# Attention and FFN on one core: the first block of x prepared in halves, and one query chunk of batch 1 loaded by itself

## The chip, the cores and the metric

One core of a Trainium2 chip. The metric is the device time of one execution in microseconds (us); of several runs the median counts. The time before is 242.38 us, the median of 3 runs that lie between 241.73 and 243.09.

## The reference, cut to what matters

```python
def phi(x, c, s):                       # c, s: cos and sin of pi/2 * position / S
    r = np.maximum(x, 0.0)
    return np.concatenate([r * c, r * s], axis=-1)
q_p, k_p = phi(q, cos_w, sin_w), phi(k, cos_w, sin_w)   # (8, 8, 576, 128)
kv  = np.einsum('bhsf,bhsd->bhfd', k_p, v)
z   = np.sum(k_p, axis=2)
num = np.einsum('bhsf,bhfd->bhsd', q_p, kv)
den = np.einsum('bhsf,bhf->bhs', q_p, z)[..., None] + 1e-06
x   = (num / den).transpose(0, 2, 1, 3).reshape(4608, 512)
out = ((x @ w1) * (x @ w2)) @ w3 @ w_out                # w1, w2: 512 x 1024
```

Linear attention over 8 batches (576 rows, 8 heads of 64) makes x, and a multiplicative FFN takes it. The kernel multiplies w3 by w_out once (w34) and works in bf16.

## The kernel before, in words

A batch is cut into five chunks: four of 128 rows (0 to 3) and one of 64 (4). A row index in a chunk is a partition; which row of the batch that is follows from the load, which gives each partition 5 (or 4) neighbouring rows of a head, and output rows go back by the same map. Batch 0's queries and all of batch 7 are loaded whole; the others in two parts, rows 0 to 319 to partitions 0 to 63 and rows 320 to 575 to partitions 64 to 127.

For a batch, the features of k and q (`prep_k`, `prep_q`, both through `features`) are made on VectorE (cosine half, L506, sometimes the sine half, L514) and ScalarE (sine half, L511); `prep_v` copies v beside a column of ones (L526). `kv` multiplies features of k by v over the chunks (L561; for an odd batch chunk 4 comes first), `num` multiplies the transposed features of q by that (L596), `norm` divides (L607 to L609) into `xblk`, and x is transposed into `xT` by TensorE and a copy (`x_tr`, L638 and L639) or by a DMA. Batch 0 has functions of its own in the first 17 us (L956, L964). The FFN takes 512 columns of `xT` at a time (`ffn_groups`): products with w1 and w2 (L685), a copy `asb` (L709, L728, L745), a product of the two on VectorE (L711, L735, L751), then the product with w34 (L768) or seven smaller ones (L878). The FFN's first tile takes its first 128 columns, then the next 128, from `xT` (L696): chunk 0 and chunk 1 of batch 0. `w34_mm` (L483) makes w34 from `w3T`, which `w3_tr` transposes on VectorE (L473) as w3 arrives.

The order of all work on all engines is a table, `PLAN`: a name and its arguments per step, in the order in which the steps are issued. `f t` is the next step of the FFN's generator for tile t, `l b name part` a load, `xt` an `x_tr`, `qt` transposes of q's features, `qy` one half of a copy that a `qt` left out, `idle n` puts n matmuls on zeros (L466) into TensorE's queue. Every engine works through its own steps strictly in that order. Loads are issued by GpSimd (L384), in the same queue as its copies of v. A DMA that GpSimd issues counts on one of eight semaphores in turn, and its issue waits until the DMA that used this semaphore before, eight DMAs earlier, has landed; GpSimd's later steps wait behind it.

```python
    def load_rows(eng, t, rows, half):
        j, span = (5, slice(0, 320)) if half == 0 else (4, slice(320, S))
        eng.dma_start(out=t[ts(half, 64), :, 0:j, :].rearrange("p h j d -> p h (j d)"),
                      in_=rows[:, span, :].rearrange("h (p j) d -> p h (j d)", j=j))
```

Of the kernel before, what the change touches and what calls it, by code (L numbers as in the profile page):

```python
# [16 lines left out]
P = 128  # L17
# [22 lines left out]
f 0; t3 0  # L40
f 0; lg 2 q 0; t3 1; l 2 k 0; l 2 k 1; l 2 q 1; l 2 v 0
f 0
# [25 lines left out]
f 0  # L68
f 0; n 1 0; d 1 0; xt 1 4 A; q 2 0 0; q 2 1; lt 3 v 0; xt 0 4 A
f 0  # L70
f 0; v 2 0 G
f 0
f 0; xt 1 0 V; n 1 1
f 0
# [204 lines left out]


def out_rows(b, c):

    if c < 4:
        return slice(0, 128)
    return slice(64, 128) if b % 2 == 0 else slice(0, 64)


def _angles(nc, pool):

    s_i = pool.tile([P, 2 * NCH], I32, name="s_i")  # L290
    nc.gpsimd.iota(s_i[0:64, 0:5], pattern=[[1, 5]], base=0, channel_multiplier=5)
    nc.gpsimd.iota(s_i[64:128, 0:5], pattern=[[1, 5]], base=320, channel_multiplier=4)
# [30 lines left out]
def kernel(  # L323
# [56 lines left out]

    def load_rows(eng, t, rows, half):

        j, span = (5, slice(0, 320)) if half == 0 else (4, slice(320, S))
        eng.dma_start(out=t[ts(half, 64), :, 0:j, :].rearrange("p h j d -> p h (j d)"),  # L384
                      in_=rows[:, span, :].rearrange("h (p j) d -> p h (j d)", j=j))
# [68 lines left out]
    nc.vector.memset(kp_bufs[0][64:128, 4, :, :], 0.0)  # L454
    nc.vector.memset(raw[0, "v"][64:128, :, 4, :], 0.0)
    clear_rows(0)
# [60 lines left out]
    def prep_k(b, c, n=H, **kw):  # L517
        features(att_of(b)["kp"], raw[b, "k"][:, :, c, :], c, NCH + c if b == 7 else c, n, **kw)

    def prep_q(b, c, n=H, **kw):  # L520
        rows = raw[b, "q"][:, :, c, :] if b > 0 else q0f[:, :, c, :] if c < 4 else q04[:]
        features(att_of(b)["qp"], rows, c, NCH + c if b in WHOLE else c, n, **kw)

    def prep_v(b, c, copy=None):
        R = ROWS[c]
        (copy or nc.gpsimd.tensor_copy)(out=att_of(b)["va"][:R, c, :, 0:D], in_=raw[b, "v"][:R, :, c, :])  # L526

# [72 lines left out]
    def norm(b, c, g0=0, ng=2):  # L600
        rows, R = out_rows(b, c), ROWS[c]
        n4 = att[b]["n"][c][rows, g0:g0 + ng, 0:260].rearrange("p g (h e) -> p g h e", e=65)
        if g0 == 0:
            att[b]["x"][c] = sm.tile([P, 2, 4, D], BF16, name="xblk", bufs=6)
        xblk = att[b]["x"][c]
        den = sm.tile([P, 2, 4], FP32, name="den")
        nc.vector.tensor_scalar_add(out=den[rows, 0:ng], in0=n4[:, :, :, 64], scalar1=1e-6)  # L607
        nc.vector.reciprocal(out=den[rows, 0:ng], in_=den[rows, 0:ng])
        nc.vector.tensor_tensor(out=xblk[rows, g0:g0 + ng], in0=n4[:, :, :, 0:D],  # L609
                                in1=den[rows, 0:ng].unsqueeze(3).to_broadcast([R, ng, 4, D]),  # L610
                                op=ALU.mult)
        divided[0] = xblk[rows, 0, 0, 0:1]
# [20 lines left out]
    def x_tr(b, c, copy=None):  # L633
# [5 lines left out]
        (copy or nc.scalar.copy)(out=x_place(b, c), in_=pst[:, 0:4, 0:R])  # L639

    held = []
    newest = [None]

    def rows_of(b, c, n):
# [6 lines left out]
        upper = out[ds(b * S + 320, 256), :].rearrange("(p j) m -> p j m", j=4)  # L651
        return [h[:, c:c + n, :] for h in ((lower,) if c == 4 else (lower, upper))]

# [22 lines left out]
    def ffn_groups(t):  # L676
# [267 lines left out]
    def kv_first(c, sums, *which):  # L944
# [71 lines left out]
    def store_behind_transposes():  # L1016
# [6 lines left out]
        "f": lambda t: next(ffn[t]), "w": w34_mm, "w3": load_w3, "wo": load_wout, "w12": w12,  # L1023
        "l": load, "lg": gated, "lt": behind_transposes, "lx": behind_division, "lk": behind_feature, "q04": load_q04, "gx": behind_first_x,
        "k": prep_k, "q": prep_q, "v": prep_v,
# [3 lines left out]
        "n": num, "n0": num_first,  # L1029
        "d": norm, "xt": x_tr, "xd": x_dma, "idle": idle_mms, "open": open_ffn, "second": second_pair, "more": more_banks,  # L1030
        "clear": clear_rows, "tw": weight_block, "t3": w3_tr, "st": store_next, "ss": store_by_sync,
# [37 lines left out]
```

## Time and profile before

| | |
|---|---|
| median of 3 runs | 242.38 us (241.73 to 243.09) |
| the profiled execution's own time | 242.14 us |
| its span, first to last instruction | 240.4 us |
| TensorE busy | 234.1 us, 97% of the span |
| VectorE, ScalarE, GpSimd busy | 190.5, 115.6, 79.9 us |
| first FFN product (L685) | 16.90 us |
| `kv` of batch 1 starts (L561) | 50.60 us |
| mean granted TensorE clock | 0.997 |

The span starts at the first instruction, and all times in the trace count from there. A line of the timeline gives start, duration, engine, source line, what is written from what, shape and type, the count of merged instructions, and in square brackets how long the engine had sat idle and what ended that. PE is TensorE, PEld its weight loads, DVE VectorE, ACT ScalarE, POOL GpSimd; POOLq is GpSimd's sequencer.

### The profile page before, as it was taken

How to read it: one execution, taken by the hardware profiler on the slowest of the kernel's cores; microseconds unless marked ns; L12 is line 12 of the kernel's file. 1: busy time of each engine (PE TensorE's matmuls, PEld its weight loads, DVE VectorE, ACT ScalarE, POOL GpSimd, SP SyncE). 2: the span in 40 equal slices, each digit the busy share in tenths (PEclk: the TensorE clock that was granted, in tenths of full speed). 3: DMA queues.
4: the chain of work that ended last, by engine and by line, in shares of the span. 5: the costliest groups of instructions: out<-in, count | busy, mean ns of one | idle time of the engine just before them, and what ended most of it. 6: DMA issues, size and time to landing. Idle time of an engine off the chain costs nothing.

```text
span 240.4 us, 5811 instructions
## 1 busy us (share of the span) xinstructions
PE 234.1 (97%) x2236; PEld 163.5 (68%) x2236; DVE 190.5 (79%) x462; ACT 115.6 (48%) x203; POOL 79.9 (33%) x149
## 2 busy tenths in 40 slices
PE   8999999999999999999999999999999999999993
PEld 2579545476964585798588859966985797484462
DVE  6774596968988937999799889998999788785560
ACT  2754314687755732775384436447164312313321
POOL 8663888541804231221431222021020050363020
PEclk9999999999999999999999999999999999999998
DMA  7999999999999999599999999788457739599824
GB/s 195 194 196 199 183 189 187 198 199 192 182 195 136 142 151 219 76 183 175 148 188 170 152 158 169 131 129 77 80 196 133 110 85 156 130 303 327 253 72 176
DMA packets 84939, 40.48 MB, mean 168 GB/s; under 512 B 48048, under 2 KB 82096, under 8 KB 84912
## 3 DMA queue, kind: packets, MB, share of 16 engines
q0 software_dynamic: 37616, 23.60, 66.9%
q1 hardware_dynamic: 47152, 16.46, 38.8%
q8 instruction: 17, 0.28, 0.4%
q14 instruction: 10, 0.08, 0.2%
q10 hardware_dynamic: 144, 0.07, 0.1%
HBM read 38.80 MB, written 9.44 MB: 201 GB/s over the span
## 4 chain that ended last, share of the span: by engine, by line
PE 92%; DMA 3%; POOL 1%; ACT 1%; DVE 1%; issue 1%; POOLq 0%; DVEq 0%
PE ffnps L685 52%; PE ffnps L878 14%; PE ffnps L768 7%; PE ffnps L483 6%; PE pnum L596 4%; PE pnum L561 4%; DMA vs<-in_v_dram 3%; PE ffnmore L878 1%; PE pst L578 1%; PE ffnps L811 1%; PE ffnps L786 1%; PE pst L638 1%; POOL kf L384 1%; ACT qpT L582 0%; PE pnum L956 0%
## 5 line engine op out<-in xcount | busy, mean ns | idle before, releaser
L685 PE MATMUL ffnps<-xT,w1b 128*128 128x256 bf16 (+2 forms) x448 | 76.2, 303 | 0.2
L685 PE MATMUL ffnps<-xT,w2b 128*128 128x256 bf16 (+2 forms) x448 | 76.2, 303 | 0.0
L685 PEld LDWEIGHTS <-w1b 128*128 128x128 bf16 x448 | 41.1, 98 | 19.3 <-issue 0.8
L685 PEld LDWEIGHTS <-w2b 128*128 128x128 bf16 x448 | 40.8, 98 | 19.7 <-issue 0.2
L745 ACT CAST asb<-ffnps 128x512 bf16<-128x512 f32 x40 | 23.4, 586 | 43.2 <-PE ffnps L685 39.0
L751 DVE TENSOR_TENSOR abT<-asb,ffnps 128x512 bf16<-128x512 bf16 x40 | 27.2, 683 | 15.8 <-PE ffnps L685 15.5
L728 ACT CAST asb<-ffnps 128x512 bf16<-128x512 f32 x24 | 14.1, 586 | 32.9 <-PE ffnps L685 25.9
L609 DVE TENSOR_TENSOR xblk<-pnum,den 128x512 bf16<-128x512 f32 (+1 forms) x38 | 26.2, 691 | 1.5
L735 DVE TENSOR_TENSOR abT<-asb,ffnps 128x512 bf16<-128x512 bf16 x24 | 16.2, 681 | 7.2 <-PE ffnps L685 7.2
L511 ACT ACTIVATE kp<-kf,sinv 128x512 bf16<-128x512 bf16 (+4 forms) x33 | 21.0, 663 | 1.3 <-DMA kf<-in_k_dram 1.3
L878 PEld LDWEIGHTS <-abT 128*128 128x128 bf16 x192 | 18.5, 98 | 3.2
L427 POOL COPY seen<-asb 128x1 bf16<-128x1 bf16 x15 | 3.2, 213 | 50.8 <-ACT asb L728 45.9
L511 ACT ACTIVATE qp<-qs,sinv 128x512 bf16<-128x512 bf16 (+6 forms) x31 | 18.7, 630 | 2.1 <-DMA qs<-in_q_dram 2.1
L596 PEld LDWEIGHTS <-qpT 128*128 128x128 bf16 x320 | 15.1, 98 | 4.3 <-DVE xblk L609 0.4
L768 PE MATMUL ffnps<-w34b,abT 128*128 128x512 bf16 x72 | 17.5, 379 | 0.0
L596 PE MATMUL pnum<-kvs,qpT 128*128 128x65 bf16 x304 | 15.7, 194 | 0.0
L878 PEld LDWEIGHTS <-s 128*128 128x128 bf16 x144 | 13.9, 98 | 1.6
L506 DVE TENSOR_SCALAR kp<-kf,cosv 128x512 bf16<-128x512 bf16 (+1 forms) x40 | 14.5, 384 | 0.4 <-DMA kf<-in_k_dram 0.4
L483 PE MATMUL ffnps<-early,w3T 128*128 128x512 bf16 x64 | 14.3, 379 | 0.0
L384 POOL DMA_DIRECT2D vs<-in_v_dram x16 | 11.9, 750 | 3.5 <-DMA kf<-in_k_dram 1.6
L878 PE MATMUL ffnps<-w34b,abT 128*128 128x256 bf16 x96 | 12.4, 273 | 0.0
L506 DVE TENSOR_SCALAR qp<-qs,cosv 128x512 bf16<-128x512 bf16 (+1 forms) x35 | 12.1, 356 | 0.1
(147 smaller groups left out, 334.1 us busy)
## 6 DMA issues: line engine op xcount, KB each, us to landing
out_dram<-osb SPq DMA_DIRECT2D x9, 256.0 KB, 3.4
kf<-in_k_dram POOLq DMA_DIRECT2D x7, 320.0 KB, 7.0
early<-in_moe_w_dram POOLq DMA_DIRECT2D x16, 128.0 KB, 5.1
qs<-in_q_dram POOLq DMA_DIRECT2D x6, 320.0 KB, 7.6
vs<-in_v_dram POOLq DMA_DIRECT2D x6, 320.0 KB, 7.1
kf<-in_k_dram POOLq DMA_DIRECT2D x7, 256.0 KB, 8.7
qs<-in_q_dram POOLq DMA_DIRECT2D x6, 256.0 KB, 6.8
vs<-in_v_dram POOLq DMA_DIRECT2D x6, 256.0 KB, 8.1
```

What stands on the lines that cost most here:

```text
L384: eng.dma_start(out=t[ts(half, 64), :, 0:j, :].rearrange("p h j d -> p h (j d)"), in_=rows[:, span, :].rearrange("h (p j) d -> p h (j d)", ...
L483: nc.tensor.matmul(acc[:, :], lhsT=w3T[:, lc, :], rhs=woutb[:, lc, :], start=(lc == 0), stop=(lc == 7))
L506: nc.vector.tensor_scalar(out=dst[:R, c, :, 0:D], in0=rows[:R], scalar1=0.0, scalar2=cosv[:R, at:at + 1], op0=ALU.max, op1=ALU.mult)
L511: nc.scalar.activation(out=dst[:R, c, 0:n, D:F], in_=rows[:R, 0:n], func=ACTF.Relu, scale=sinv[:R, at:at + 1], bias=0.0)
L596: nc.tensor.matmul(nt[:, h // 4, ds((h % 4) * 65, 65)], lhsT=qpT[:, h, ds(at, 128)], rhs=kvs[:, h, :], start=True, stop=True)
L609: nc.vector.tensor_tensor(out=xblk[rows, g0:g0 + ng], in0=n4[:, :, :, 0:D], in1=den[rows, 0:ng].unsqueeze(3).to_broadcast([R, ng, 4, D]), ...
L685: nc.tensor.matmul(out, lhsT=w[:, kc, ts(jc, 128)], rhs=x[:, kc, tok], start=(kc == 0), stop=(kc == 3))
L735: nc.vector.tensor_mul(out=abT[:, ts(pair, 2), ts(half, 256)], in0=asb[:].rearrange("p (i n) -> p i n", i=2), in1=bT[:, :].rearrange("p (i ...
L745: nc.scalar.copy(out=asb[:], in_=aT[:, :])
L751: nc.vector.tensor_mul(out=abT[:, jc, :], in0=asb[:], in1=bT[:, :])
L768: nc.tensor.matmul(ops[:, :], lhsT=abT[:, jc, ts(ms, 128)], rhs=w34b[:, jc, :], start=(jc == 0), stop=(jc == 7))
L878: nc.tensor.matmul(into[:, ts(ms, 256)], lhsT=a[:, kc, ts(ms, 128)], rhs=b[:, kc, :], start=(ms == 0 and kc == 0), stop=(ms == 1 and kc == 3))
```

## The change

It has four parts.

1. **The first block of x in halves.** For chunks 0 and 1 of batch 0, `norm` divides by groups of four heads (two instructions of 256 columns in place of one of 512). The new `x_half` transposes two of the four column blocks and copies them to `xT` on ScalarE; it takes the place of `xt 0 0` and `xt 0 1`. Chunk 0's second half uses the PSUM bank `kva`. The FFN's first tile has one step more, after its first product with w1, so that the transposes of chunk 1's halves stand between the first products; three idle matmuls go (one of two ahead of chunk 0's transposes, both ahead of the first product), `qy 0 3 1` moves from VectorE to ScalarE, `xt 0 3` comes one FFN step earlier, and `n 0 3` and `d 0 3` move behind chunk 1.
2. **Memory order.** In batches in two parts, chunk c lies in place `(c + 1) % 5` of the loaded tile and of the five neighbouring rows, so chunk 4 comes first. The angle table's base and the stores follow.
3. **Batch 1's query chunk 3 by itself.** `l 1 q 0; l 1 q 1` become `l1q 0 4`, which loads places 0 to 3 (chunks 4, 0, 1, 2), again as two DMAs; `l1q 4 5` loads place 4 (chunk 3) as two DMAs of 64 columns, behind batch 2's keys and ahead of `l 2 q 1`.
4. **Later features.** `q 1 3` (chunk 3's features, before with both halves on VectorE) moves from ahead of batch 1's keys to behind `d 1 0`, with its sine half on ScalarE, and `q 2 1` moves behind `n 1 1`.

```diff
+BY_GROUP = ((0, 0), (0, 1))
...
+def place_of(c):
+
+    return (c + 1) % NCH
...
-    def load_rows(eng, t, rows, half):
+    def load_rows(eng, t, rows, half, places=(0, 5)):
...
-        eng.dma_start(out=t[ts(half, 64), :, 0:j, :].rearrange("p h j d -> p h (j d)"),
-                      in_=rows[:, span, :].rearrange("h (p j) d -> p h (j d)", j=j))
+        a, b = max(places[0], half), places[1]
+        eng.dma_start(out=t[ts(half, 64), :, a:b, :].rearrange("p h j d -> p h (j d)"),
+                      in_=rows[:, span, :].rearrange("h (p j) d -> p h j d", j=j)[:, :, a - half:b - half]
+                      .rearrange("p h j d -> p h (j d)"))
...
+    def load_q1(*places):
+
+        if places[0] == 0:
+            raw[1, "q"] = ld.tile([P, H, NCH, D], BF16, name="qs", bufs=NRQ)
+        for half in range(2):
+            load_rows(nc.gpsimd, raw[1, "q"], q[1], half, places)
...
-        nc.vector.tensor_tensor(out=xblk[rows, g0:g0 + ng], in0=n4[:, :, :, 0:D],
...
+        n = 1 if (b, c) in BY_GROUP else ng
+        for g in range(0, ng, n):
+            nc.vector.tensor_tensor(out=xblk[rows, g0 + g:g0 + g + n], in0=n4[:, g:g + n, :, 0:D],
...
+    first_x = []
+
+    def x_half(c, half):
+
+        if not first_x:
+            first_x.append(ps_tr.tile([P, 8, 128], BF16, name="pst"))
+        pst = first_x[0]
+        if c == 0 and half == 1:
+            pst = kva[:, :].bitcast(BF16).rearrange("p (k r) -> p k r", k=8)
+        xf = att[0]["x"][c][:].rearrange("p g h d -> p (g h d)")
+        for kc in (2 * half, 2 * half + 1):
+            nc.tensor.transpose(pst[:, kc, :], xf[:, ts(kc, 128)], identb[:])
+        nc.scalar.copy(out=x_place(0, c)[:, ts(half, 2)], in_=pst[:, ts(half, 2), :])
...
+                                if t == 0 and half == 0 and quarter == 0 and i == 0 and w is w1b:
+                                    yield
```

Three places show what this does to the order. The first is GpSimd's queue from batch 1's value loads on (`vs` are values, `kf` keys, `qs` queries; the last two `vs` rows of each are the loads of batch 2's values, and the `va_95` copy behind them is chunk 4 of batch 1's v, which `kv 1` reads first). In brackets stand the semaphores that a row waits for. Before:

```order
L384 DMA vs<-in_v_dram 64x8x320 [waits DMASW3_49]
L384 DMA vs<-in_v_dram 64x8x256 [waits DMASW4_49]
L427 COPY seen<-asb 128x1 [waits Activation_49]
L384 DMA qs<-in_q_dram 64x8x320 [waits DMASW5_49]
L384 DMA kf<-in_k_dram 64x8x320 [waits DMASW6_49,DVE_49]
L384 DMA kf<-in_k_dram 64x8x256 [waits DMASW7_49]
L384 DMA qs<-in_q_dram 64x8x256 [waits DMASW0_49]
L384 DMA vs<-in_v_dram 64x8x320 [waits DMASW1_49,PE_49]
L384 DMA vs<-in_v_dram 64x8x256 [waits DMASW2_49]
L526 COPY va_95<-vs 64x8x64 [waits DMASW3_49]
```

And with the change:

```order
L391 DMA vs<-in_v_dram 64x8x320 [waits DMASW3_49]
L391 DMA vs<-in_v_dram 64x8x256 [waits DMASW4_49]
L442 COPY seen<-asb 128x1 [waits Activation_49]
L391 DMA qs<-in_q_dram 64x8x320 [waits DMASW5_49]
L391 DMA kf<-in_k_dram 64x8x320 [waits DMASW6_49,DVE_49]
L391 DMA kf<-in_k_dram 64x8x256 [waits DMASW7_49]
L391 DMA qs<-in_q_dram 64x8x64 [waits DMASW0_49]
L391 DMA qs<-in_q_dram 64x8x64 [waits DMASW1_49]
L391 DMA qs<-in_q_dram 64x8x256 [waits DMASW2_49]
L391 DMA vs<-in_v_dram 64x8x320 [waits DMASW3_49,PE_49]
L391 DMA vs<-in_v_dram 64x8x256 [waits DMASW4_49]
L542 COPY va_95<-vs 64x8x64
```

Two DMAs stand in the queue that were not there. So batch 2's last value load, ahead of the copy of v, now waits for semaphore 4, which batch 1's own second value load raises when it lands; before it waited for semaphore 2, which batch 1's second key load raises.

The second place is VectorE between the first division and the first product of the FFN (`den` and `xblk` are `norm`'s, from the PSUM tiles `pfirst` and `pnum`; the copy to `qpT` is `qy 0 3 1`). Before:

```order
L608 RECIPROCAL den<-den 128x8
L609 TENSOR_TENSOR xblk<-pfirst,den 128x512
L607 TENSOR_SCALAR den<-pnum 128x8
L608 RECIPROCAL den<-den 128x8
L609 TENSOR_TENSOR xblk<-pnum,den 128x512
L587 COPY qpT_96<-pst 128x4x128
```

And with the change:

```order
L624 RECIPROCAL den<-den 128x8
L627 TENSOR_TENSOR xblk<-pfirst,den 128x256 x2
L623 TENSOR_SCALAR den<-pnum 128x8
L624 RECIPROCAL den<-den 128x8
L627 TENSOR_TENSOR xblk<-pnum,den 128x256 x2
L623 TENSOR_SCALAR den<-pfirst 128x8
```

Each 512-wide division has become two of 256, and the copy is gone from VectorE. The third place is ScalarE at the same point (`qpT` from `pst` is `qy 0 3`, `xT` the transposed x). Before:

```order
L587 COPY qpT_96<-pst 128x4x128
L639 COPY xT<-pst 128x4x128 x2
L709 CAST asb<-ffnps 128x512
L639 COPY xT<-pst 128x4x128
L709 CAST asb<-ffnps 128x512 x3
```

And with the change:

```order
L603 COPY qpT_96<-pst 128x4x128
L671 COPY xT<-pst 128x2x128
L671 COPY xT<-kva 128x2x128
L603 COPY qpT_96<-pst 128x4x128
L671 COPY xT<-pst 128x2x128 x2
L746 CAST asb<-ffnps 128x512
```

Two whole copies of x have become four half ones, with the second half of `qy 0 3` between them.

More of the change, by code (lines that the diff above doesn't have):

```diff
@@ L40 @@
 f 0; t3 0
-f 0; lg 2 q 0; t3 1; l 2 k 0; l 2 k 1; l 2 q 1; l 2 v 0
+f 0; lg 2 q 0; t3 1; l 2 k 0; l 2 k 1; l1q 4 5; l 2 q 1; l 2 v 0
 f 0
@@ L72 @@
 f 0
-f 0; xt 1 0 V; n 1 1
+f 0; xt 1 0 V; n 1 1; q 2 1
 f 0
@@ L517, in prep_k @@
     def prep_k(b, c, n=H, **kw):
[L518 removed]
+        features(att_of(b)["kp"], raw[b, "k"][:, :, c if b == 7 else place_of(c), :], c,
+                 NCH + c if b == 7 else place_of(c), n, **kw)
     def prep_q(b, c, n=H, **kw):
[L521 to L522 removed]
+        rows = raw[b, "q"][:, :, c if b == 7 else place_of(c), :] if b > 0 else q0f[:, :, c, :] if c < 4 else q04[:]
+        features(att_of(b)["qp"], rows, c, NCH + c if b in WHOLE else place_of(c), n, **kw)
     def prep_v(b, c, copy=None):
         R = ROWS[c]
[L526 removed]
+        (copy or nc.gpsimd.tensor_copy)(out=att_of(b)["va"][:R, c, :, 0:D], in_=raw[b, "v"][:R, :, c if b == 7 else place_of(c), :])
     transposed = [None]
@@ L639, in x_tr @@
         (copy or nc.scalar.copy)(out=x_place(b, c), in_=pst[:, 0:4, 0:R])
+    first_x = []
[9 more added lines that the diff above has]
+        nc.scalar.copy(out=x_place(0, c)[:, ts(half, 2)], in_=pst[:, ts(half, 2), :])
+        if half == 1:
+            att[0]["x"].pop(c)
     held = []
@@ L651, in rows_of @@
         upper = out[ds(b * S + 320, 256), :].rearrange("(p j) m -> p j m", j=4)
-        return [h[:, c:c + n, :] for h in ((lower,) if c == 4 else (lower, upper))]
+        at = place_of(c)
+        return [lower[:, at:at + n, :]] + ([upper[:, c:c + n, :]] if c < 4 else [])
     def store(eng, osb, g, n, cols=slice(0, DM)):
@@ L1023 @@
         "f": lambda t: next(ffn[t]), "w": w34_mm, "w3": load_w3, "wo": load_wout, "w12": w12,
-        "l": load, "lg": gated, "lt": behind_transposes, "lx": behind_division, "lk": behind_feature, "q04": load_q04, "gx": behind_first_x,
+        "l": load, "l1q": load_q1, "lg": gated, "lt": behind_transposes, "lx": behind_division, "lk": behind_feature, "q04": load_q04, "gx": behind_first_x,
         "k": prep_k, "q": prep_q, "v": prep_v,
@@ L1029 @@
         "n": num, "n0": num_first,
-        "d": norm, "xt": x_tr, "xd": x_dma, "idle": idle_mms, "open": open_ffn, "second": second_pair, "more": more_banks,
+        "d": norm, "xt": x_tr, "xh": lambda b, c, half: x_half(c, half), "xd": x_dma, "idle": idle_mms, "open": open_ffn, "second": second_pair, "more": more_banks,
         "clear": clear_rows, "tw": weight_block, "t3": w3_tr, "st": store_next, "ss": store_by_sync,
```

24 lines of the change are left out of this document (12 added, 12 removed).

## The prediction

> **What bounds the kernel now.** I read the page's totals first, then the groups by line for the time after the start, then the timeline where TensorE still waits.
>
> ```profile
> PE 234.1 (97%) x2236; PEld 163.5 (68%) x2236; DVE 190.5 (79%) x462; ACT 115.6 (48%) x203; POOL 79.9 (33%) x149
> PE 92%; DMA 3%; POOL 1%; ACT 1%; DVE 1%; issue 1%; POOLq 0%; DVEq 0%
> ```
>
> TensorE is busy in all of the span but some 6 us. The groups by line between 22.6 and 236.4 us say where those 6 us are not (last column: idle before the instructions):
>
> ```profile
> L685 PE MATMUL ffnps<-xT,w1b 128*128 128x256 bf16 (+2 forms) x416 | 72.9, 308 | 0.1
> L596 PE MATMUL pnum<-kvs,qpT 128*128 128x65 bf16 x288 | 14.8, 194 | 0.0
> L561 PE MATMUL pnum<-va,kp 128*128 128x65 bf16 x280 | 10.0, 193 | 0.0
> ```
>
> No group shows more than 0.1 us. So behind 22.6 us there is nothing to win, only to lose: what makes TensorE wait there is paid in full. What can be won lies ahead of 22.6 us, and is kept only if every engine that TensorE meets later is early enough too. The change takes no useful matmul away.
>
> **Part 1, the first block of x.** The timeline before, from the first division:
>
> ```profile
> 14.92 0.69 DVE L609 TENSOR_TENSOR xblk<-pfirst,den 128x512 bf16<-128x512 f32 x1
> 15.67 0.40 PE L638 MATMUL pst<-identb,xblk 128*128 128x128 bf16 x4
> 16.10 0.59 ACT L639 COPY xT<-pst 128x512 bf16<-128x512 bf16 x1 [0.48 <-PE pst L638]
> 16.90 0.38 PE L685 MATMUL ffnps<-xT,w1b 128*128 128x128 bf16 x4
> 17.77 0.59 ACT L639 COPY xT<-pst 128x512 bf16<-128x512 bf16 x1 [1.08 <-PE pst L638]
> 18.41 0.38 PE L685 MATMUL ffnps<-xT,w1b 128*128 128x128 bf16 x4
> 22.14 0.42 DVE L639 COPY xT<-pst 128x512 bf16<-128x512 bf16 x1
> 22.16 0.39 PE L685 MATMUL ffnps<-xT,w2b 128*128 128x128 bf16 x4
> 22.61 0.38 PE L685 MATMUL ffnps<-xT,w1b 128*128 128x128 bf16 x4
> ```
>
> The links are division, 0.06 to the transposes, copy, 0.21 to the product. At 18.41 and 22.61 TensorE has waited again for a copy to `xT`, the second time since the four matmuls at 22.16, 0.056 apart, were through at 22.38. A division of 256 columns from PSUM has no row; it lies between half of 0.69 and 0.69, and I take 0.42, since these two VectorE groups show that halving 1024 to 512 saves 0.27:
>
> ```profile
> L858 DVE TENSOR_TENSOR s<-abT,s 128x1024 bf16<-128x1024 bf16 x6 | 4.1, 685 | 0.0
> L858 DVE TENSOR_TENSOR s<-abT,s 128x512 bf16<-128x512 bf16 x13 | 5.5, 424 | 0.4
> L639 ACT COPY xT<-pst x6: 352/586/591, 16.1 to 62.3; 128x512 bf16<-128x512 bf16 x4, 128x256 bf16<-128x256 bf16 x2
> ```
>
> A copy of half the columns takes 0.35 (the third row's minimum). Two transposes take 0.3, by the 0.40 of four less two steps. So the first half is divided at 14.92 + 0.42 = 15.34, transposed by 15.70 and copied by 16.06; the second is divided at 15.69, transposed by 16.06 and copied by 16.42, and the products that need it start at 16.63. Before, they came two matmuls behind 16.90, at 17.01: 0.38 earlier. Two later waits of TensorE go: some 0.1 at 18.41 for chunk 1, whose copies now end at 17.9, when its products start, and 0.23 ahead of 22.61, since `xt 0 3` comes a step earlier. The lead at 22.61 is about 0.7 us; if the halves cost as much as the wholes, only 0.2 remains. The idle matmuls fill a wait and are worth nothing; `qy 0 3 1` on ScalarE ends at 17.0 and is first read at 17.7.
>
> **How much of the lead is kept to 50 us.** VectorE transposes w3 as it lands, and loads don't start earlier because TensorE does:
>
> ```profile
> 33.79 0.41 PEld L483 LDWEIGHTS <-w3T 128*128 128x128 bf16 x3 [0.24 <-DVE w3T L473]
> 37.44 1.30 DVE L473 STREAM_TRANSPOSE w3T<-early 128x512 bf16<-128x512 bf16 x2 [1.93 <-DMA early<-in_moe_w_dram]
> 39.16 1.23 DVE L473 STREAM_TRANSPOSE w3T<-early 128x1024 bf16<-128x1024 bf16 x1
> 40.57 0.42 DVE L582 COPY qpT<-pst 128x512 bf16<-128x512 bf16 x1 [0.18 <-PE pst L578]
> 41.24 0.42 PE L596 MATMUL pnum<-kvs,qpT 128*128 128x65 bf16 x8
> ```
>
> VectorE is tied to a landing at 37.44 and works on to 40.39; the copy at 40.57 can come 0.18 earlier and no more, and the matmul at 41.24, which reads it, begins 0.25 behind its end at 40.99, of which I leave 0.07 for the way between engines. So of 0.7 us 0.18 + 0.18, about 0.35, is kept here; the first row shows a weight load waiting for the same chain at 33.79, where some of it goes already. TensorE would then reach `kv 1` at 50.60 - 0.35 = 50.25.
>
> **Parts 2 and 4.** The new places move the same bytes in runs of the same length. `q 1 3` leaves two instructions of VectorE's queue ahead of `kv 1`, each issued 0.26 behind the last, so features and copies of v there come 0.5 earlier:
>
> ```profile
> 46.40 0.34 DVE L506 TENSOR_SCALAR qp<-qs,cosv 128x512 bf16<-128x512 bf16 x1
> 46.66 0.34 DVE L514 TENSOR_SCALAR qp<-qs,sinv 128x512 bf16<-128x512 bf16 x1
> 50.36 1.04 DVE L526 COPY va<-vs 128x512 bf16<-128x512 bf16 x4
> 50.60 1.44 PE L561 MATMUL pnum<-va,kp 128*128 128x65 bf16 x40
> ```
>
> Without that, the copies at 50.36, read chunk by chunk from 50.85 on, would be late for an earlier `kv 1`. Behind `d 1 0` the features of `q 1 3` are due only for `qt 1 3`, eight FFN steps later; this I cost at nothing. `l 3 q 0`, which overwrites the tile, now waits for them, and GpSimd stands in that wait, but it stood idle there until 59.35 for batch 2's values anyway:
>
> ```profile
> 59.35 0.62 POOL L526 COPY va<-vs 128x512 bf16<-128x512 bf16 x1 [8.64 <-DMA vs<-in_v_dram]
> 66.69 1.27 PE pnum L561 x40
> ```
>
> **Part 3, the added wait.** GpSimd around the same place:
>
> ```profile
> 36.77 0.68 POOL L384 DMA_DIRECT2D qs<-in_q_dram  x1
> 40.56 0.68 POOL L384 DMA_DIRECT2D vs<-in_v_dram  x1 [1.04 <-DMA early<-in_moe_w_dram]
> 44.59 0.68 POOL L384 DMA_DIRECT2D qs<-in_q_dram  x1 [0.31 <-DMA qs<-in_q_dram]
> 46.53 0.74 POOL L384 DMA_DIRECT2D vs<-in_v_dram  x1 [1.27 <-DMA kf<-in_k_dram]
> 47.60 1.80 POOL L384 DMA_DIRECT2D vs<-in_v_dram  x1 [0.33 <-DMA kf<-in_k_dram]
> 49.39 0.62 POOL L526 COPY va<-vs 64x512 bf16<-64x512 bf16 x1
> 49.95 0.76 POOL L384 DMA_DIRECT2D qs<-in_q_dram  x1
> ```
>
> The load at 47.60 is `l 2 v 1`, the copy at 49.39 is `v 1 4`, chunk 4 of batch 1's v, and `kv 1` begins with chunk 4. In the changed queue `l 2 v 1` waits for the landing of `l 1 v 1`. The loads by issue window give the time to landing of three loads: `l 1 q 1` (issued at 36.77), `l 1 v 1` (at 40.56) and `l 2 v 1` itself (at 47.60):
>
> ```profile
> qs<-in_q_dram POOLq DMA_DIRECT2D x1, 256.0 KB, 7.5
> vs<-in_v_dram POOLq DMA_DIRECT2D x1, 256.0 KB, 9.7
> vs<-in_v_dram POOLq DMA_DIRECT2D x1, 256.0 KB, 11.6
> ```
>
> They land at 44.27, 50.26 and 59.20. From the second to the third come six loads of 1728 KB (three of 320, three of 256), so 5.2 ns per KB; `l1q 0 4` is 128 KB smaller, so `l 1 v 1` lands 0.66 earlier, at 49.60. From a landing to the issue that waited for it pass about 0.3 (44.27 to the row at 44.59, which waited for that one). Then `l 2 v 1` is issued at 49.9, which takes 0.68 to 1.80; I take 0.76, the nearest row, at 49.95, beside the same copies of v on VectorE. `v 1 4` starts at 50.65 and takes 0.62, and `kv 1` starts behind it at 51.3 in place of 50.60. TensorE waits about 1.05 us there, and everything behind is **0.7 us later than before**; whatever part 1 won is gone, since this wait hangs on a landing and not on TensorE. By the extremes: 0.6 at the shortest issue, 1.75 at the longest, and -0.35 if `v 1 4` were ready in time. The small loads themselves cost little: they carry what the large ones no longer do, and batch 2's values land within half a microsecond of 59.2, with `kv 2` at 66.69, the row above.
>
> **The sum.** Own time 242.14, plus 0.7 is 242.8; the profiled execution lies 0.24 below the median of the runs, so against that median I predict 242.38 + 0.7 = **243.1 us**.
>
> **Rivals.**
> *The long issue.* The issue at 47.60 took 1.80 while VectorE ran features without a gap. If `l 2 v 1` meets that again, `kv 1` starts at 52.35 and the time is 242.38 + 1.75 = 244.1. For it: VectorE's copies of v become free to run at the same landing that starts this issue, so the two meet each time. Against it: of all issues of this line between 36 and 51 us one alone took so long. The Trainium skill, "SBUF — State Buffer", section "SBUF: two separate sides", says that VectorE and GpSimd share a pair of ports as an exclusive lock, so that GpSimd can't write the descriptors of its DMAs while some VectorE operations run. The row at 47.60 agrees, the row at 49.95 (0.76) only in part; by that rule the issue would end behind the last copy of v, and this rival weighs more.
> *The gain is kept.* `v 1 4` decides only if it ends later than 50.25; a wait for `l 1 v 1` that ended by 48.8 would spare it. Then the time is 242.38 - 0.35 = 242.0, or 241.7 if all 0.7 us survive. For it: TensorE waits for nothing there now. Against it: the landing at 50.26 would have to move by 1.7, and 0.66 is what the bytes give.
> *The clock.* TensorE has less to do between 15 and 17 us, by three idle matmuls; were its clock granted at half for the products from 16.9 to 22.6, this would cost between nothing and 5.7 us, say 2.9, or 245.3. Against it:
>
> ```profile
> 9.00:10.00 1.00, 0.61 (x9) 0.43 (x7) 1.00 (x3) 1.00 (x3) 0.52 (x1) 1.00 1.41 197
> 15.00:17.00 2.00, 1.76 (x23) 0.81 (x20) 1.93 (x6) 1.21 (x3) 0.57 (x2) 1.00 1.44 198
> ```
>
> The first number behind the stretch's length is TensorE's busy time, the third from the end its clock: 0.61 of a microsecond sufficed for 1.00, and the changed kernel stays near that. The Trainium skill, "TensorE: Matmul & The Clock Gate", "Part 1: The HAM clock gate", puts the idle time that throttles at about 3.4 us; no wait here comes near.
> *The change does less than it says.* If the second half's products wait as long as before, the start gains nothing; the end is the same, since `v 1 4` decides it.
>
> **How the numbers follow.** The forecast (0.4 to 1.2 later) has 0.47, the long issue (1.2 to 2 later) 0.28, the kept gain (0.4 later to 0.7 earlier) 0.21, the clock 0.04. 0.5% is 1.2 us, about what a measurement of this kernel can tell from no change. Slower by more: the long issue, the clock, and 0.05 of the forecast, 0.37. Faster by more needs 1.2 us, which no term gives; with the scatter of the runs 0.03. Within: 0.60. The range, from the kept gain to the long issue with a little scatter, is 241.7 to 244.3, for 8 in 10.
>
> **What would show it.** The first product near 16.3, its second half near 16.6; a weight load of `w34_mm` waiting for `w3T`, or the matmul of 41.24 for its copy; then TensorE idle for about a microsecond ahead of the first `kv` matmul at 50.3, ended by GpSimd's copy, and GpSimd's `l 2 v 1` waiting for a DMA of `vs` until 49.9. If `kv 1` starts at or ahead of 50.6, part 3 is wrong; if TensorE waits anew behind 52 us, I have missed a wait.

## The result, and the profile after

| | before | after |
|---|---|---|
| median of 22 runs | 242.39 us | 244.72 us |
| lowest and highest | 241.73, 246.66 | 242.18, 248.56 |
| ratio, 95% interval | | 1.0058 (1.0035 to 1.0080) |
| the profiled execution's own time | 242.14 us | 245.92 us |
| its span | 240.4 us | 244.0 us |
| TensorE busy | 234.1 us | 233.1 us |

The ratio leaves out executions that lie more than 1.5% above the fastest of their kernel (six of the changed kernel, the profiled one among them, and one of the kernel before), while the median counts all. By the ratio the changed kernel takes 242.39 x 1.0058 = 243.8 us, inside the predicted range; the plain median lies 0.4 us above the range. The changed kernel is slower by 1.4 to 2.3 us, where 0.7 was forecast, and its executions scatter more.

TensorE's waits behind 22 us say where that time is; the kernel before had none there (waited for: us in total, times, longest):

```profile
PE pnum L612 <- DMA qpT<-qp: 2.8, 3, 1.5
PE pnum L577 <- POOL va L542: 1.0, 1, 1.0
PE ffnps L805 <- DVE abT L788: 0.2, 1, 0.2
```

The second row is the forecast wait at `kv 1`. The first was not forecast: TensorE waits three times for transposed features of queries (`qpT`), which SyncE's queue moves by DMA. TensorE's timeline shows the places:

```profile
40.77 0.43 PE L612 MATMUL pnum<-kvs,qpT 128*128 128x65 bf16 x8
...
51.31 1.43 PE L577 MATMUL pnum<-va,kp 128*128 128x65 bf16 x40 [1.00 <-POOL va L542]
...
77.38 0.43 PE L612 MATMUL pnum<-kvs,qpT 128*128 128x65 bf16 x8 [0.33 <-DMA qpT<-qp]
...
79.68 0.42 PE L612 MATMUL pnum<-kvs,qpT 128*128 128x65 bf16 x8 [1.01 <-DMA qpT<-qp]
...
144.14 0.43 PE L612 MATMUL pnum<-kvs,qpT 128*128 128x65 bf16 x8 [1.50 <-DMA qpT<-qp]
```

The start of the changed kernel, from the timeline (DVE, ACT and PE):

```profile
14.88 0.76 DVE L627 TENSOR_TENSOR xblk<-pfirst,den 128x256 bf16<-128x256 f32 x2
15.69 0.37 ACT L671 COPY xT<-pst 128x256 bf16<-128x256 bf16 x1
16.02 0.37 ACT L671 COPY xT<-kva 128x256 bf16<-128x256 bf16 x1
16.11 0.60 PE L720 MATMUL ffnps<-xT,w1b 128*128 128x128 bf16 x4
...
22.08 0.39 PE L720 MATMUL ffnps<-xT,w1b 128*128 128x128 bf16 x4
```

Two divisions in 0.76, copies of 0.37, the first product at 16.11 and not at 16.90: part 1 does what it says. The products that began at 22.61 now begin at 22.08, a lead of 0.53.

GpSimd's rows around `kv 1` (its timeline; L391 is a load, L542 a copy of v):

```profile
46.94 1.89 POOL L391 DMA_DIRECT2D qs<-in_q_dram  x1 [0.24 <-DMA kf<-in_k_dram]
48.81 0.68 POOL L391 DMA_DIRECT2D vs<-in_v_dram  x1
49.88 0.68 POOL L391 DMA_DIRECT2D vs<-in_v_dram  x1 [0.38 <-DMA vs<-in_v_dram]
50.55 0.71 POOL L542 COPY va<-vs 64x512 bf16<-64x512 bf16 x1
57.61 0.68 POOL L391 DMA_DIRECT2D qs<-in_q_dram  x1 [6.34 <-DVE qp L529]
59.51 0.62 POOL L542 COPY va<-vs 128x512 bf16<-128x512 bf16 x1 [1.22 <-DMA vs<-in_v_dram]
```

`l 2 v 1` waits for a landing and goes out at 49.88, `v 1 4` is copied at 50.55. The fifth row is `l 3 q 0`: it stood for 6.34 us behind the moved features of `q 1 3`, and left at 57.61 in place of 49.95. What the DMA engines did meanwhile, in stretches of 2 us (stretch: length, busy time of PE, PEld, DVE, ACT, POOL, TensorE's clock, DMA share, GB/s), first before:

```profile
56.00:58.00 2.00, 2.00 (x21) 1.09 (x19) 1.97 (x7) 1.70 (x4) 0.00 (x0) 1.00 1.43 197
58.00:60.00 2.00, 2.00 (x40) 1.95 (x39) 1.55 (x6) 1.28 (x3) 0.65 (x2) 1.00 1.76 185
60.00:62.00 2.00, 2.00 (x35) 1.91 (x33) 1.82 (x3) 1.10 (x2) 2.00 (x5) 1.00 0.92 174
```

and after:

```profile
56.00:58.00 2.00, 2.00 (x20) 1.17 (x20) 1.73 (x6) 2.00 (x5) 0.39 (x1) 1.00 1.26 173
58.00:60.00 2.00, 1.95 (x31) 1.53 (x29) 1.93 (x6) 1.17 (x4) 0.78 (x2) 1.00 0.43 27
60.00:62.00 2.00, 2.00 (x34) 1.93 (x31) 1.93 (x6) 1.29 (x3) 2.00 (x5) 1.00 1.18 166
```

The last column is what to see: 27 GB/s in place of 185. Over the six microseconds 2 x (197 + 185 + 174) - 2 x (173 + 27 + 166), about 380 KB, were not moved, 2 us of work at 190 GB/s. It comes later. Of batch 3's values the first part goes out at almost the same time in both (59.90 and 60.06) and lands 5.4 us after its issue before, and 8.9 after the change; the last part of its keys (issued at 64.51 and 65.75) 6.9 and 11.1 (the loads of two windows: KB, us to landing), before:

```profile
vs<-in_v_dram POOLq DMA_DIRECT2D x1, 320.0 KB, 5.4
kf<-in_k_dram POOLq DMA_DIRECT2D x1, 256.0 KB, 6.9
```

and after:

```profile
vs<-in_v_dram POOLq DMA_DIRECT2D x1, 320.0 KB, 8.9
kf<-in_k_dram POOLq DMA_DIRECT2D x1, 256.0 KB, 11.1
```

So these loads run into the time of the transposes. The transposes of query features between 56 and 82 us, issues and time to landing, before:

```profile
L534 SPq DMA_TRANSPOSE qpT<-qp x7: 1231/1339/2192, 57.3 to 80.7; - x7
...
DMA to landing us min/median/max: 4.3/5.4/6.7
```

and after:

```profile
L550 SPq DMA_TRANSPOSE qpT<-qp x6: 1231/2175/4434, 57.7 to 79.4; - x6
...
DMA to landing us min/median/max: 5.1/7.7/9.7
```

The median from issue to landing rose from 5.4 to 7.7 us (the window holds one transpose more before; without it the median is 5.4 too). By the timelines `kv 2` starts at 67.23 (before 66.53, so 0.70 later), `kv 3` at 85.38 (before 82.90, so 2.48 later): 1.78 were lost between the two. In this execution another 1.68 goes at 144 us; no experiment's profile has that, and its cause stays open. Without it the profiled time would be near 244.2, close to the median.

Those three, 0.70, 1.78 and 1.68, are all that TensorE loses: the last store is issued 4.16 us later (timeline, before and after).

```profile
236.71 0.37 ACTq L670 DMA_DIRECT2D out_dram<-osb  x1
240.87 0.37 ACTq L705 DMA_DIRECT2D out_dram<-osb  x1
```

The span is only 3.6 us longer, since from that issue to its end pass 3.69 us before and 3.13 after. The experiments below show the same: 3.34 to 3.75 in the six profiles of kernels built on the kernel before, 3.08 to 3.17 in the six built on the changed kernel. So the changed kernel gains about half a microsecond behind its last store. No experiment was made on why.

### The profile page after: what moved, and what is told of

Same layout as the page of the kernel before. It is cut to its first block, busy times and chain, and to the rows that moved or that the text cites. A ratio compares the mean times of both kernels' runs of the same rounds, so it can differ in the third digit from the quotient of the medians.

```text
span 244.0 us, 5792 instructions
## 1 busy us (share of the span) xinstructions
PE 233.1 (96%) x2213; PEld 163.0 (67%) x2233; DVE 189.7 (78%) x462; ACT 116.7 (48%) x207; POOL 81.8 (34%) x151
## 4 chain that ended last, share of the span: by engine, by line
PE 69%; DMA 23%; POOL 4%; issue 1%; SPq 1%; ACT 0%; DVE 0%; POOLq 0%
PE ffnps L720 40%; PE ffnps L915 14%; DMA qpT<-qp 7%; DMA early<-in_moe_w_dram 5%; PE ffnps L805 5%; DMA w2b<-in_moe_w_dram 4%; DMA vs<-in_v_dram 4%; PE pnum L612 4%; PE pnum L577 3%; DMA kf<-in_k_dram 3%; PE ffnmore L915 1%; POOL early L430 1%; POOL w1b L1021 1%; PE ffnps L848 1%; SPq L550 1%
## 5 line engine op out<-in xcount | busy, mean ns | idle before, releaser
L720 PE MATMUL ffnps<-xT,w1b 128*128 128x256 bf16 (+2 forms) x435 | 75.2, 301 | 0.6
L627 DVE TENSOR_TENSOR xblk<-pnum,den 128x512 bf16<-128x512 f32 (+2 forms) x39 | 26.3, 677 | 1.5
L526 ACT ACTIVATE qp<-qs,sinv 128x512 bf16<-128x512 bf16 (+6 forms) x32 | 19.6, 634 | 4.7 <-DMA qpT<-qp 3.0
L805 PE MATMUL ffnps<-w34b,abT 128*128 128x512 bf16 x68 | 16.8, 379 | 0.3 <-DVE abT L788 0.2
L391 POOL DMA_DIRECT2D qs<-in_q_dram x14 | 11.2, 800 | 9.4 <-DVE qp L529 6.3
L521 DVE TENSOR_SCALAR kp<-kf,cosv 128x512 bf16<-128x512 bf16 (+1 forms) x40 | 14.0, 374 | 0.0
```

The source lines that it names most:

```text
L521: nc.vector.tensor_scalar(out=dst[:R, c, :, 0:D], in0=rows[:R], scalar1=0.0, scalar2=cosv[:R, at:at + 1], op0=ALU.max, op1=ALU.mult)
L526: nc.scalar.activation(out=dst[:R, c, 0:n, D:F], in_=rows[:R, 0:n], func=ACTF.Relu, scale=sinv[:R, at:at + 1], bias=0.0)
L627: nc.vector.tensor_tensor(out=xblk[rows, g0 + g:g0 + g + n], in0=n4[:, g:g + n, :, 0:D], in1=den[rows, g:g + n].unsqueeze(3).to_broadcast( ...
L720: nc.tensor.matmul(out, lhsT=w[:, kc, ts(jc, 128)], rhs=x[:, kc, tok], start=(kc == 0), stop=(kc == 3))
L805: nc.tensor.matmul(ops[:, :], lhsT=abT[:, jc, ts(ms, 128)], rhs=w34b[:, jc, :], start=(jc == 0), stop=(jc == 7))
```

## The experiments

Ten kernels in twelve runs, each timed beside the kernel before on the same chip. The theory: two losses, the wait at `kv 1` and the late `l 3 q 0`. The rival: DMA transposes vary from execution to execution by themselves, and the late load costs nothing.

**Two small loads alone (e1_two_small).** The kernel before, and:

```diff
+    def two_small():
+        for i in range(2):
+            nc.gpsimd.dma_start(out=spare[0:1, ts(i, 64)], in_=q[1, 0, i:i + 1, :])
-... l 2 k 1; l 2 q 1; l 2 v 0
+... l 2 k 1; two; l 2 q 1; l 2 v 0
```

> The kernel before, with two loads of 128 bytes each, which nothing reads, put into GpSimd's queue between batch 2's keys and `l 2 q 1`; everything else as before. First theory (the changed kernel loses at two places: at `kv 1` through the shift of GpSimd's eight landing semaphores, and behind 57 us through the late `l 3 q 0`): only the first loss is here. `l 2 v 1` waits for the landing of `l 1 v 1` at 50.26, is issued near 50.55, `v 1 4` is copied near 51.25 and `kv 1` starts near 51.95 in place of 50.60. TensorE shows one wait of 1.3 us for that copy and none for the transposes of query features; `l 3 q 0` is issued behind the copy, near 51.9, and the DMA engines have no gap. Ratio 1.005 to 1.006. Rival (the shift of the semaphores isn't the cause, `kv 1` came late because of the bytes or the order of the loads): `kv 1` stays at 50.6, ratio 0.999 to 1.001.

Measured: median 243.06 against 242.29, ratio 1.0016 (0.9983 to 1.0050). TensorE's one wait, and GpSimd's timeline (L384 a load, L533 the copy):

```profile
PE pnum L568 <- POOL va L533: 1.3, 1, 1.3
```

```profile
50.12 1.38 POOL L384 DMA_DIRECT2D vs<-in_v_dram  x2
51.49 0.71 POOL L533 COPY va<-vs 64x512 bf16<-64x512 bf16 x1
52.93 0.68 POOL L384 DMA_DIRECT2D qs<-in_q_dram  x1 [0.72 <-DMA qs<-in_q_dram]
```

Two loads of 128 bytes that nothing reads put `kv 1` at 52.26, 1.66 later, 1.25 of it the wait for the copy: the wait comes from their place in the queue, not from bytes or from memory order. It came in another way than expected, though. The first row holds both loads of batch 2's values without a gap, so no wait of `l 2 v 1` for a landing is seen here; ahead of them the issue of `l 2 q 1` began at 47.88 and took 2.24. In that profile own time rose by 1.36; in the medians only 0.77 is left, less than the ratio of 1.005 to 1.006 that was expected, and the ratio cannot tell it from nothing.

**Late features, and with them the late load (e2_late_feature).** Part 4 alone on the kernel before:

```diff
-w 5 4 4; q 1 3 0
+w 5 4 4
-... xt 1 4 A; q 2 0 0; q 2 1; lt 3 v 0
+... xt 1 4 A; q 1 3; q 2 0 0; lt 3 v 0
-f 0; xt 1 0 V; n 1 1
+f 0; xt 1 0 V; n 1 1; q 2 1
```

> The kernel before, with the features of `q 1 3` (and of `q 2 1`) moved behind `d 1 0` as in the change; loads, memory order and start as before. So `l 3 q 0`, which overwrites the tile that `q 1 3` reads, waits, and nothing shifts the semaphores. First theory (two losses): `kv 1` at 50.1 to 50.6, without a new wait; `l 3 q 0` is issued near 57 instead of 49.95, GpSimd's loads behind it follow only then, the DMA engines run empty between about 59 and 61 and batch 3's loads land 2 to 3 us later, among the transposes of batch 2's query features; TensorE waits 0.5 to 3 us for `qpT` between 75 and 82 us. Ratio 1.002 to 1.010. Rival (the time of those transposes varies by itself from execution to execution, and the late load costs nothing, as the prediction had it): no new wait of TensorE but what the kernel before also has, ratio 0.998 to 1.001.

Measured: median 245.34, ratio 1.0087 (1.0049 to 1.0124). The wait is there, and so is the hole in the DMA (waits, then the stretch):

```profile
PE pnum L596 <- DMA qpT<-qp: 1.0, 1, 1.0
```

```profile
58.00:60.00 2.00, 1.81 (x34) 1.57 (x32) 1.63 (x7) 1.55 (x4) 0.83 (x3) 1.00 0.46 29
```

Part 4, which the prediction costed at nothing, is by itself as slow as the whole change.

**The load released (e5_own_tile, e5b_own_tile).** The changed kernel, but `l1q 4 5` fills a tile of 1 KB in each partition, `q13`, which `q 1 3` reads. `l 3 q 0` then overwrites nothing that is still to be read.

```diff
+    q13 = const.tile([P, H, D], BF16, name="q13")
-        rows = raw[b, "q"][:, :, c if ...
+        rows = q13[:] if (b, c) == (1, 3) else raw[b, "q"][:, :, c if ...
```

> The changed kernel, with the two small loads of batch 1's fourth query chunk put into a tile of their own (1 KB in each partition), which `q 1 3` reads; so `l 3 q 0` no longer waits for the features of `q 1 3`. The shift of the semaphores stays. First theory (two losses): `kv 1` still at 51.3, 0.7 late; `l 3 q 0` is issued near 51.5 and lands near 61, the DMA engines don't run empty, no wait of TensorE for `qpT` near 77 to 80. Ratio 1.001 to 1.004, with no more scatter than the kernel before. Rival (the transposes vary by themselves): the ratio stays at the changed kernel's 1.0058, and the waits for `qpT` with it.

Measured: median 242.42, ratio 0.9983 (0.9954 to 1.0012). The load leaves at 52.01, the DMA engines stay full, and one wait is left (timeline, stretch, waits):

```profile
52.01 0.68 POOL L391 DMA_DIRECT2D qs<-in_q_dram  x1 [0.54 <-DVE va L548]
```

```profile
58.00:60.00 2.00, 2.00 (x34) 1.53 (x31) 1.88 (x6) 1.17 (x3) 0.28 (x1) 1.00 1.49 210
```

```profile
PE pnum L583 <- POOL va L548: 1.2, 1, 1.2
```

The waits for `qpT` are gone and the rival with them: nothing in the transposes was changed.

**Both losses undone (e6_both, e6b_both).** The same, and `v 1 4 G` ahead of `l 2 v 1`:

```diff
-w 6 4 4; q 1 2 4; k 1 4 0; l 2 v 1; v 1 4 G
+w 6 4 4; q 1 2 4; k 1 4 0; v 1 4 G; l 2 v 1
```

> As the kernel with the tile of its own for the fourth chunk, and `v 1 4` copied ahead of the issue of `l 2 v 1` in GpSimd's queue, so that it waits only for its own values. First theory (two losses, both undone here): `v 1 4` starts near 49.9, `kv 1` near 50.6 (0.25 to 0.35 later than TensorE could start it, no later than in the kernel before), no wait for `qpT`; `l 2 v 1` issued near 50.6, hidden by the loads ahead of it. Ratio 0.998 to 1.001. Rival (the loss lies elsewhere, in the transposes or in the small loads): ratio 1.003 to 1.006.

Measured: median 242.41, ratio 0.9982 (0.9947 to 1.0017). In its profile VectorE waited for the last of w3 until 42.61, a microsecond longer than in e5_own_tile (41.60), TensorE waited 0.6 us for those transposes, and `kv 1` started at 51.35 without a wait for the copy. So this kernel and the one before it ran again side by side:

> The kernel with the tile of its own for the fourth chunk again, for more runs beside the next one. First theory: 0.5 to 0.8 us over the next one, since its `kv 1` waits for the issue of `l 2 v 1`. Rival (that wait is given back later, or the other kernel meets an equal one): both within 0.2 us.

> The kernel with the tile of its own and with `v 1 4` copied ahead of the issue of `l 2 v 1`, again, for more runs beside the one before it. First theory: ratio 0.996 to 0.999, `kv 1` at 50.2 to 50.7 where the last of w3 lands as in the kernel before (near 41.4; it landed at 42.5 in the first profile of this kernel). Rival: as the one before it, 0.998 to 1.001.

Measured: 242.91, ratio 1.0020 (0.9999 to 1.0041), and 242.56, ratio 0.9993 (0.9967 to 1.0019). Now `kv 1` starts without a wait (TensorE's timeline of e6b_both):

```profile
50.67 1.43 PE L583 MATMUL pnum<-va,kp 128*128 128x65 bf16 x40
```

against 51.74 in the profile beside it, and the spans are 239.9 and 241.0. The medians of the two pairs differ by 0.01 and 0.35, less than the 0.5 to 0.8 that was expected, and in e1_two_small by 0.77. The wait at `kv 1` is thus real in the traces; what it is worth in the time of many runs these pairs don't resolve. In the traces it is not given back: in e5_own_tile `kv 2` starts 0.91 us later than in the kernel before, and the last store is issued at 237.63 in place of 236.71, still 0.92 later. Its span is only 0.4 us longer, because of the shorter stretch behind the last store. That these kernels are no slower than the kernel before therefore doesn't mean that the wait costs nothing. Neither version beats the kernel before by more than its interval.

**Part 1 alone (e3_start_only).** The kernel before with the halves and the start of the plan.

> The kernel before with part 1 alone: x of the first two chunks divided, transposed and copied in halves, and the start of the plan that goes with it; loads, memory order and `q 1 3` as before. First theory (part 1 wins a lead, the loads keep about 0.35 us of it): the matmul of 41.24 comes at 40.7 to 40.9, `kv 1` at 50.1 to 50.4, no new wait; ratio 0.997 to 0.9995. Rival (the lead is lost at the landing of w3 or of batch 1's values): `kv 1` at 50.5 to 50.7, ratio 0.9995 to 1.001.

Measured: median 242.75 against 242.43, ratio 1.0012 (0.9997 to 1.0026). `kv 1` starts at 50.11, as expected, and no gain arrives. The timeline shows where it goes:

```profile
56.61 0.35 DVE L507 TENSOR_SCALAR qp<-qs,cosv 128x512 bf16<-128x512 bf16 x1 [0.58 <-DMA qs<-in_q_dram]
...
58.16 0.69 DVE L612 TENSOR_TENSOR xblk<-pnum,den 128x512 bf16<-128x512 f32 x1
...
58.91 0.43 PE L597 MATMUL pnum<-kvs,qpT 128*128 128x65 bf16 x8 [0.22 <-DVE xblk L612]
```

VectorE waits for batch 2's queries to land, its division behind them starts no earlier than before, and TensorE waits for that division. `kv 2` starts at 66.50, before at 66.53: the lead of 0.49 at `kv 1` is given back within nine microseconds, at a landing.

**Which of the two in part 4 (e8_late_load).** On the kernel before, the load alone is held, by a copy of one element, until the division `d 1 0`:

```diff
-... qt 1 2 A; l 3 q 0; v 2 2 G; v 1 0 V
+... qt 1 2 A; v 1 0 V
-... xt 1 4 A; q 2 0 0
+... xt 1 4 A; lx 3 q 0; v 2 2 G; q 2 0 0
```

> The kernel before, with one thing moved: `l 3 q 0` waits, by a copy of one element to `seen`, for the division `d 1 0` (near 56.6 us) and so is issued near 57.2 in place of 49.95. No feature, start, tile or other load is changed, and `kv 1` isn't touched. First theory (the late load, with the DMA engines running empty before it, is the loss behind 57 us): the same loss as with the moved features, ratio 1.005 to 1.012, 27 GB/s or little more in 58 to 60 us, and waits of TensorE for `qpT` between 75 and 82 or near 140 in the profile. Rival (in that kernel the features of `q 1 3` and `q 2 1`, moved on VectorE and ScalarE, delayed the transposes themselves): ratio 0.999 to 1.002.

Measured: median 242.81, ratio 1.0013 (0.9997 to 1.0030). The expectation of the first theory was missed. The stretch and the transposes (56 to 82 us) lie between the cases:

```profile
58.00:60.00 2.00, 2.00 (x42) 2.00 (x41) 1.58 (x5) 1.40 (x3) 0.77 (x2) 1.00 0.68 57
```

```profile
DMA to landing us min/median/max: 5.5/7.0/9.3
```

The transposes already take 7.0 and not 5.4, and TensorE loses 0.54 us between `kv 2` and `kv 3`. So either the moved features add a share (A: in e2_late_feature the first transpose was issued at 57.54 and not at 57.26), or 0.35 us more of lateness makes the difference (B).

**The order of the features (e9_other_order, e10_after_order).** In e2_late_feature and in the changed kernel, `q 1 3` behind `q 2 0`:

```diff
-... xt 1 4 A; q 1 3; q 2 0 0; lt 3 v 0
+... xt 1 4 A; q 2 0 0; q 1 3; lt 3 v 0
```

> The kernel before with the features of `q 1 3` moved behind `d 1 0` as in the second run (`q 2 1` too), but behind those of `q 2 0` and not ahead of them; one VectorE operation changes its place, by 0.26 us. `l 3 q 0` waits as long as there or a little longer. Theory two A (the late load alone is within the slack, as the run with the late load alone had it; what takes the rest is that the transposes of batch 2's first queries are issued 0.3 to 0.4 us later, 57.54 and 58.98 in place of 57.26 and 58.71, and then stand behind batch 3's values in the DMA engines): transposes issued at 57.1 to 57.3 and 58.6 to 58.7, ratio 1.000 to 1.003, like the late load alone. Theory two B (it is the lateness of the load, and the run with the late load alone got away with 0.35 us less of it): ratio 1.006 to 1.012, as in the second run.

> The changed kernel with the same one change of order: `q 1 3` behind `q 2 0` and not ahead of it. Theory two A: ratio 1.001 to 1.004, that is the added wait at `kv 1` (0.7 us) and a little; transposes issued near 57.4 and 58.9 (the kernel is 0.15 late there by its wait at 51 us), no wait of TensorE for `qpT` of over 0.5 us between 76 and 81. Theory two B: the ratio of the changed kernel, 1.0035 to 1.008, with its waits.

Measured: 245.27 (six executions), ratio 1.0115 (1.0071 to 1.0159), and 244.98, ratio 1.0085 (1.0052 to 1.0117). In the second kernel the transposes are issued from 57.3 on as A wanted, and the wait stays (tile view, then waits):

```profile
L550 SPq DMA_TRANSPOSE qpT<-qp x6: 1232/1862/4723, 57.3 to 79.9; - x6
```

```profile
PE pnum L612 <- DMA qpT<-qp: 1.0, 1, 1.0
```

So A falls; `l 3 q 0` goes out 0.42 us later here (58.03), and the loss is no smaller. The first kernel's profile can't decide it: w3 landed late there, `kv 1` started at 52.30 and the transposes were issued from 58.4 on.

**Lateness alone (e12_later_load, e13_own_tile_late).** The first holds the load alone, on the kernel before, as the late-load kernel did, but behind `q 2 1`; the second holds it in the kernel with the tile of its own, where nothing else does:

```diff
-... xt 1 4 A; q 2 0 0; q 2 1; lt 3 v 0
+... xt 1 4 A; q 2 0 0; q 2 1; lk 3 q 0; v 2 2 G; lt 3 v 0
```

> The kernel before with `l 3 q 0` alone moved, as in the run with the late load alone, but behind the features of `q 2 1` (a copy of one element to `seen`) and so issued near 57.9 in place of 57.11; no feature, tile or start changed. Lateness alone: the loss grows steeply with the time of that issue (the four kernels so far: 57.11 gave 1.0013, 57.46 gave 1.0087, 57.61 gave 1.0058, 58.03 gave 1.0085), so ratio 1.005 to 1.010 here, with waits for `qpT` or with transposes landing 3 us late. Lateness together with the moved features (both are needed): ratio 1.000 to 1.003, as with 57.11.

> The kernel with the tile of its own for the fourth chunk, where nothing holds `l 3 q 0` back, with the load held back on purpose: behind the features of `q 2 0` (a copy of one element to `seen`), so that it is issued near 57.6 as in the changed kernel. If the tile of its own helped by the time of that load: the changed kernel's ratio, 1.004 to 1.009, and waits for `qpT`. If it helped in another way (the separate tile, the memory order of the small loads): ratio 0.998 to 1.003, as without the hold.

Measured: 244.44 (seven executions), ratio 1.0072 (1.0046 to 1.0098), and 243.94, ratio 1.0048 (1.0026 to 1.0071). The first one's waits, and its stretches:

```profile
PE pnum L596 <- DMA qpT<-qp: 1.0, 1, 1.0
PE ffnps L768 <- DVE abT L751: 0.9, 1, 0.9
```

```profile
58.00:60.00 2.00, 2.00 (x35) 1.71 (x33) 1.58 (x6) 0.99 (x3) 1.18 (x3) 1.00 0.79 140
60.00:62.00 2.00, 2.00 (x34) 1.91 (x32) 1.92 (x5) 1.46 (x3) 2.00 (x5) 1.00 0.76 71
```

Only the time of one load of 320 KB differs from the kernel before, and of what stands behind it in GpSimd's queue, and the whole loss is there. In the second, the tile of its own no longer helps once the load is held; it went out at 59.73 in that profile, where 57.6 was planned, since `kv 1` started at 53.06. Both expectations of B are met. All profiles together, in the order of that issue:

| kernel | `l 3 q 0` issued | `kv 1` | `kv 2` | `kv 3` | `kv 2` to `kv 3` | ratio |
|---|---|---|---|---|---|---|
| e3_start_only | 49.29 | 50.11 | 66.50 | 83.06 | 16.56 | 1.0012 |
| before | 49.95 | 50.60 | 66.53 | 82.90 | 16.37 | |
| e6b_both | 51.54 | 50.67 | 66.59 | 82.96 | 16.37 | 0.9993 |
| e5_own_tile | 52.01 | 51.52 | 67.44 | 83.81 | 16.37 | 0.9983 |
| e5b_own_tile | 52.38 | 51.74 | 67.66 | 84.03 | 16.37 | 1.0020 |
| e1_two_small | 52.93 | 52.26 | 68.18 | 84.55 | 16.37 | 1.0016 |
| e6_both | 53.02 | 51.35 | 67.60 | 84.08 | 16.48 | 0.9982 |
| e8_late_load | 57.11 | 50.45 | 66.41 | 83.32 | 16.91 | 1.0013 |
| e2_late_feature | 57.46 | 50.52 | 66.91 | 84.62 | 17.71 | 1.0087 |
| after | 57.61 | 51.31 | 67.23 | 85.38 | 18.15 | 1.0058 |
| e10_after_order | 58.03 | 51.21 | 67.13 | 85.98 | 18.85 | 1.0085 |
| e12_later_load | 58.45 | 50.88 | 66.96 | 85.71 | 18.75 | 1.0072 |
| e9_other_order | 59.13 | 52.30 | 68.22 | 86.05 | 17.83 | 1.0115 |
| e13_own_tile_late | 59.73 | 53.06 | 69.19 | 86.50 | 17.31 | 1.0048 |

Up to 53.02 the way from `kv 2` to `kv 3` takes 16.4 to 16.6 us, from 57.11 on 16.9 to 18.9. It is a step with scatter, not a line; why 57.11 costs so much less than 57.46 stays open. It isn't lateness against the kernel's own course: counted from its own `kv 1`, the load goes out 6.66 us later in e8_late_load and 6.30 in the changed kernel, which loses more. So a late load is enough for the loss (e12_later_load), and the moved features without a late load cost nothing there (e5_own_tile, 16.37 as before); whether they add a share beside a late load isn't shown.

## Why the prediction was right and wrong

**Nothing to win behind 22.6, and what bounds.** Right for TensorE: no version won more than its interval, and the places where it falls behind are waits of its own or of its weight loads. Not covered: the half microsecond that the changed kernel gains behind its last store, where TensorE has nothing left to do.

**Part 1.** Right at the start, not on the way. The lead at 22.61 was 0.53, forecast about 0.7. The landing of w3 was to take half of it and took almost nothing: at 41.24 the lead was 0.47, forecast 0.35. TensorE would have reached `kv 1` near 50.14 (its last products ahead of it start at 49.28 in place of 49.74, and in the kernel before `kv 1` began 0.86 behind them), forecast 50.25; that these lie so close is two errors against each other.

**Part 3.** The wait came as forecast: issue at 49.88 (49.9), copy at 50.55 (50.65), `kv 1` at 51.31 (51.3), a wait of 1.00 (1.05), and 0.70 of delay still stands at `kv 2`. Two 128-byte loads bring a wait for the same copy. In the time of many runs the pairs that differ in it alone give 0.01, 0.35 and 0.77, and don't resolve it.

**Parts 2 and 4.** Here the prediction failed, at "`l 3 q 0`, which overwrites the tile, now waits for them, and GpSimd stands in that wait, but it stood idle there until 59.35 for batch 2's values anyway". GpSimd's idleness was true and beside the point. What was queued behind its issue was work of the DMA engines: in the kernel before, no load was issued between that one, at 49.95, and the next, at 59.90, and the engines still moved 185 GB/s from 58 to 60 us. Without it they moved 27, batch 3's loads landed 3.7 and 5.4 us later, and the transposes that TensorE reads at 77 to 80 us came late with them. That the load's time is the cause is shown (the load held alone: 1.0013 at 57.11, not to be told from nothing, and 1.0072 at 58.45; released: 0.9983 and 1.0020; held again: 1.0048). That it works through the shared DMA engines is read from the stretches and the landings, and was not tested apart. The step should have said what the DMA engines do between the last landing of batch 2 and the next issue.

**The rivals.** The long issue of `l 2 v 1` did not come, 0.68 us. A gain kept as far as `kv 1`, as the one run with part 1 alone had it, is worth nothing at the end, so that rival's 242.0 was wrong too: in that profile the next landing takes it. The clock stayed at 1.00 in the profiled execution. The time came near the long issue's 244.1, by another mechanism. That it lies in the range is luck: the 0.7 at `kv 1` was foreseen, the 1.78 between `kv 2` and `kv 3` and the gain behind the last store were not.

## What to carry to other kernels

When an issue of a load is moved, cost it on the DMA engines as well as on the issuing queue: look at the stretch in which its bytes moved before, and whether anything else is queued there. A load that reuses a tile is tied to the tile's last reader; moving that reader moves the load and what waits behind it in the queue, which a small tile for the late part avoids. A lead that the start wins is worth what is left of it behind the next landing, and is read there, not at the start.

## What the runs showed of the hardware

One load issue between 46.6 and 48.7 us was long in thirteen of the fourteen profiles, 1.80 to 2.64 us, whichever load it was: `l 2 q 1` in the changed kernel (1.89, the row at 46.94), `l 2 v 1` before. In e12_later_load none was: the two issues from 46.85 on took 1.76 together. The long ones stand beside VectorE's run of features without a gap, but that alone doesn't make an issue long: before, the issue at 46.53 stands beside the same run (45.11 to 50.44) and took 0.74. The Trainium skill, "SBUF — State Buffer", "SBUF: two separate sides", has GpSimd locked out of a shared port pair while some VectorE operations run; the long issues agree with it, and the one at 46.53 doesn't show it. The issue at 49.88, beside VectorE's four copies of v (from 49.69 to 51.42), took 0.68, which speaks against the reading of that rule in the prediction, by which these copies would hold the issue.

Loads can be dear by their count: in e1_two_small, 256 bytes in two loads made TensorE wait for 1.25 us at `kv 1`.
